# A linear-attention and SwiGLU block on one core: the first token tiles and first products put in one written order

## The chip, the cores and the metric

One core of a Trainium2 chip runs the whole kernel. The metric is device time in microseconds (us) of one execution. All input and output tensors are float32 in HBM.

## The reference

```python
x = A_x                                  # 2048 tokens x 1024
xn = _layernorm(x, axis=-1)
s = _A_ref(xn, A_wqkv, A_wo)             # linear attention, 32 heads of 32, phi(t) = elu(t) + 1
g = _silu(_B_ref(xn, B_w1, B_w3, B_w2))  # SwiGLU, hidden width 3584
return x + s * g
```

In the attention, `kv` and `z` are sums over all tokens of `phi(k) v` and `phi(k)`. The output for a query is `phi(q) kv / (phi(q) z)`, times `wo`.

## The kernel before, in words

**Products.** Each matrix product is done by a seven-product scheme on 2 x 2 blocks: the left operand (normalised, transposed tokens) is kept as the blocks and sums A11, A12, A22, S1, S2, S3, S4, and the right operand (weights) as B11, B21, B22, T1, T2, T3, T4. Every operand is a pair of rounded float32 numbers, a high part and a low part: `split` (lines 83 to 92) has ScalarE round the source into the high part and VectorE subtract it from the source into the low part. `mm3` (94 to 99) multiplies high by high, high by low and low by high, and `product` (378) does so for four blocks of the inner dimension: twelve matmuls of 128 x 512.

**Halves.** The tokens come in two halves of 1024. A half has eight row tiles of 128 tokens. In the first half, tiles 0 to 3 give the upper row of blocks (A11 and A12, in the buffers `xa`), and tiles 4 to 7 the lower row (in `xb`). Tile i and tile 4 + i together give S1, S2, S3 and S4 for 128 columns of each operand.

**The start of the first half** is what the change touches:

- `prepare_first` (168 to 180) loads tiles 0 to 3, takes each tile's mean and variance on VectorE (`moments`, with `gather`, bn_stats twice on 512 columns, and `spread`, 140 to 151, a chain of small instructions with one square root on ScalarE), normalises on VectorE (`normalise`, 154), and transposes the blocks on TensorE with `turn_into` (156 to 163): four 128 x 128 transposes into one PSUM bank, ScalarE writes the high part, VectorE the low part.
- `prepare_rest` (192 to 210) does tile 4 + i: load, moments, normalise on VectorE, then four sums of 128 x 512 on GpSimd (203 to 206: S1, S3, S2 and S4), then the five transposed blocks S2, S3, S1, A22, S4 by `turn_into`. `behind` keeps its first steps from being issued before earlier ones.
- `gemm` with `early=True` (399 to 469) is done for the keys and values of pairs 0 and 1, called k0, v0, k1 and v1 here: B11 by A11, a copy of that into `u` on ScalarE, then B21 by A12 into the same bank, and `use` (phi for keys, a copy for values). The products with S1 to S4 and A22 follow when all four pairs of tiles are done. The first of them is T2 by S2 of k0.
- `Operands` (287 to 364) loads and splits the weights. For the four early ones a first load `w0...` of 128 columns (330) gives B11 and B21. The later load of 256 columns, `w...` (301), goes into the pool `raw`, whose two buffers first hold the tiles `xa0` (0 and 1) and `xa1` (2 and 3). So k0's load waits until tiles 0 and 1 have been transposed for the last time, and v0's until tiles 2 and 3 have been.

**What sets the order.** Each engine runs its own instructions in the order in which they were put in its queue. In the kernel before the compiler's scheduler chooses that order from program order and its own estimate of the times, apart from `tc.issue_after`, which holds an instruction behind another. All loads here go through SyncE's queue (SP). There are eight PSUM banks: a transposed block holds one until its low part is done, and an early product holds one from its first matmul to its `use`.

The sums of keys by values are kept in `kvacc` (110), zeroed on VectorE at the start. They are first added to by line 515, long after the stretch described here.

Of the kernel before, what the change touches and what calls it, by code (L numbers as in the profile page):

```python
# [22 lines left out]
def tile_linear_attention_times_swiglu(  # L23
# [39 lines left out]
    nc.gpsimd.memset(gap, 0.0)  # L63

# [3 lines left out]
    JG, NT = 4, C // (2 * P)  # L68
    FB = [(0, 8), (8, 16), (16, 22), (22, 28)]
# [13 lines left out]
    def split(pair, src=None, bias=None):  # L83
# [4 lines left out]
        if bias is None:  # L88
            nc.scalar.copy(out=hi, in_=src)
            return nc.vector.tensor_sub(out=lo, in0=src, in1=hi.bitcast(F32))  # L90
# [19 lines left out]
    kvacc = st.tile([P, ND, P], F32, tag="kvacc", bufs=1, name="kvacc")  # L110
    nc.vector.memset(kvacc, 0.0)
# [10 lines left out]
    def load_rows(rows, name):  # L122

        t = praw.tile([P, 2, D], F32, tag="raw", name=name)
        for c, r0 in enumerate(rows):
            nc.sync.dma_start(out=t[:, c], in_=x[r0:r0 + P, :])
        return t

    def moments(xs, dst):

        bs = st.tile([P, 2, 2, nc.vector.BN_STATS_DIM], F32, tag="bs", name="bs")
        for c, t in enumerate(xs):
            gather(t, bs[:, c])
        spread(bs, dst)

# [4 lines left out]
    def spread(bs, dst):  # L140
        n = dst.shape[1]
# [4 lines left out]
        nc.scalar.activation(y, v, AF.Sqrt)  # L146
        nc.vector.reciprocal(y, y)
# [20 lines left out]
    def prepare_first(A, mom):  # L168

        xs = []  # L170
        for g in range(TH // 4):
            t = load_rows([(2 * g + e) * P for e in range(2)], f"xa{g}")
            xs += [t[:, e] for e in range(2)]
            for i in (2 * g, 2 * g + 1):
                moments(xs[i:i + 1], mom[:, i:i + 1])
                normalise(xs[i], mom[:, i])
                turn_into(A, {"A11": xs[i][:, :C]}, i, f"0_{i}")
        for i, t in enumerate(xs):
            _, low = turn_into(A, {"A12": t[:, C:]}, i, f"0_{i}")
        return xs, low  # L180

    def load_second(mom, g):

        ts = []
        for i in (2 * g, 2 * g + 1):
            ts.append(job_tile([P, D], f"xb{i}") if i < 3 else pb.tile([P, D], F32, tag="b", name=f"xb{i}"))
            nc.sync.dma_start(out=ts[-1], in_=x[C + i * P:C + (i + 1) * P, :])
        j = TH // 2 + 2 * g
        moments(ts, mom[:, j:j + 2])
        return ts  # L190

    def prepare_rest(A, mom, i, t0, seconds, behind):

        with ExitStack() as order:
            for mark in behind:
                order.enter_context(tc.issue_after(mark.ins))
            if i % 2 == 0:
                seconds += load_second(mom, i // 2)
            t1, s1 = seconds[i], small(f"S1x{i}")
            normalise(t1, mom[:, TH // 2 + i])  # L200

            a11, a12, a21, a22 = t0[:, :C], t0[:, C:], t1[:, :C], t1[:, C:]
            nc.gpsimd.tensor_add(out=s1, in0=a21, in1=a22)
            nc.gpsimd.tensor_sub(out=a21, in0=a11, in1=a21)
            nc.gpsimd.tensor_sub(out=a11, in0=s1, in1=a11)
            last = nc.gpsimd.tensor_sub(out=a12, in0=a12, in1=a11)
        behind.append(last)
        yield
        turned, _ = turn_into(A, {"S2": a11, "S3": a21, "S1": s1, "A22": a22, "S4": a12}, i, f"0_{i}")
        yield turned  # L210
# [76 lines left out]
    class Operands:  # L287
# [15 lines left out]
        def upto(self, n):  # L303
            while n not in self.B:
                next(self.stages)
            return self.B[n]
# [823 lines left out]
```

## Time and profile before

| | us |
|---|---|
| median of 3 runs (2372.07 to 2375.66) | 2372.78 |
| profiled execution, its own time | 2371.04 |
| span of the profiled execution | 2369.0 |
| TensorE busy in the span | 2329.2 |

Times in the rows count from the start of the span. In a row of the timeline stand the start, the duration, the engine (PE is TensorE's matmul, DVE is VectorE, ACT is ScalarE, POOL is GpSimd, SPq the queue of SyncE), the line, the operation, what it writes and reads with the shape, how many instructions are merged in the row, and in brackets the idle time of the engine before it and what ended it. Instructions overlap in an engine's pipeline: two starts on one engine lie closer than one duration.

### The profile page before, as it was taken

The page shows a single profiled execution, that of the slowest core. Times are in us where ns is not written, and L with a number is a line of the kernel's source. Part 1 is how long each engine was busy: PE and PEld are TensorE (multiplying, and loading weights), DVE is VectorE, ACT ScalarE, POOL GpSimd, SP SyncE. Part 2 cuts the span into 40 slices and gives each one's busy share as a digit, 9 for nine tenths or more (in the row PEclk, how much of TensorE's full clock was granted, in tenths as well). Part 3 has the DMA queues.
Part 4 walks back from the last instruction along what each step waited for, and adds up shares of the span by engine and source line. Part 5 has one row for each costly group of instructions (what it writes and reads, how often), then busy time and mean ns, then how long its engine had stood idle before and what let it go on. Part 6 is the DMA issues. An engine that isn't in the chain of part 4 may idle for free.

```text
span 2369.0 us, 29756 instructions
## 1 busy us (share of the span) xinstructions
PE 2329.2 (98%) x10544; PEld 1928.1 (81%) x10544; DVE 1635.7 (69%) x2906; ACT 940.7 (40%) x1595; POOL 330.7 (14%) x423
## 2 busy tenths in 40 slices
PE   6999999999999999999999999999999999999999
PEld 5788888888888888888788888888888888878777
DVE  8755687879788675657776877777636556676644
ACT  5433544443333244445434332333535233344532
POOL 3000111212121110000131312122100111210001
PEclk9999999999999999999999999999999999999999
DMA  3222444547666573334353555543636565665656
GB/s 125 89 98 81 169 147 165 196 156 249 226 236 232 173 291 114 121 118 140 135 184 132 195 179 184 172 150 119 229 97 222 151 187 183 192 199 158 190 147 151
DMA packets 264676, 395.48 MB, mean 167 GB/s; under 512 B 20944, under 2 KB 187088, under 8 KB 264080
## 3 DMA queue, kind: packets, MB, share of 16 engines
q1 hardware_dynamic: 230416, 293.12, 38.1%
q0 software_dynamic: 34112, 100.48, 12.2%
q8 instruction: 82, 1.34, 0.2%
q14 instruction: 66, 0.54, 0.1%
HBM read 271.58 MB, written 140.77 MB: 174 GB/s over the span
## 4 chain that ended last, share of the span: by engine, by line
PE 94%; DMA 3%; DVE 1%; POOL 1%; ACT 1%; issue 0%; SPq 0%; DVEq 0%; ACTq 0%; POOLq 0%
PE cB L99 3%; PE cB L97 3%; PE cB L98 3%; PE dB L99 2%; PE dB L97 2%; PE dB L98 2%; PE aB L99 2%; PE aB L98 2%; PE aB L97 2%; PE kv L514 1%; DMA XA12s<-qs_d 1%; PE cs L97 1%; PE cs L99 1%; PE cs L98 1%; PE den L754 1%; PE ds L98 1%
## 5 line engine op out<-in xcount | busy, mean ns | idle before, releaser
L636 POOL DMA_DIRECT2D ho_d<-hs x112 | 101.7, 908 | 84.5 <-DVE hs L609 62.0
L628 POOL DMA_DIRECT2D ho_d<-sg x56 | 51.1, 912 | 432.0 <-DVE sg L623 358.1
L787 POOL DMA_DIRECT2D qs_d<-qd x32 | 27.8, 874 | 457.7 <-DVE qd L611 430.2
L587 POOL DMA_DIRECT2D pq_d<-pq x32 | 17.6, 550 | 484.9 <-DVE pq L475 480.3
L962 DVE TENSOR_TENSOR acc<-cB,acc 128x512 f32<-128x512 f32 x73 | 50.2, 688 | 20.1 <-PE cB L99 20.0
L626 POOL DMA_DIRECT2D ho_d<-sg x56 | 37.9, 677 | 135.0 <-DVE sg L623 120.6
L915 DVE TENSOR_TENSOR XA12B<-XA12B 128x512 fp32r<-128x512 f32 (+1 forms) x32 | 19.7, 624 | 45.4 <-ACT XA12B L914 45.4
L962 DVE TENSOR_TENSOR acc<-dB,acc 128x512 f32<-128x512 f32 x53 | 36.5, 688 | 19.9 <-PE dB L99 19.7
L99 PE MATMUL cB<-T3B,XS3B 128*128 128x512 f32 x112 | 43.9, 392 | 1.0 <-DVE XS3B L915 1.0
L99 PE MATMUL cB<-T4B,XA22B 128*128 128x512 f32 x112 | 43.7, 391 | 0.6 <-DVE XA22B L915 0.6
L99 PE MATMUL dB<-T1B,XS1B 128*128 128x512 f32 x112 | 43.8, 391 | 0.4 <-DVE XS1B L915 0.4
L97 PE MATMUL cB<-T2B,XS2B 128*128 128x512 f32 x112 | 44.0, 393 | 0.2
L97 PE MATMUL cB<-T3B,XS3B 128*128 128x512 f32 x112 | 43.8, 391 | 0.3 <-ACT XS3B L914 0.3
L99 PE MATMUL dB<-B22B,XS4B 128*128 128x512 f32 x112 | 43.8, 391 | 0.0
L97 PE MATMUL cB<-T4B,XA22B 128*128 128x512 f32 x112 | 43.7, 391 | 0.0
L99 PE MATMUL cB<-T2B,XS2B 128*128 128x512 f32 x112 | 43.7, 390 | 0.0
L98 PE MATMUL cB<-T4B,XA22B 128*128 128x512 f32 x112 | 43.6, 390 | 0.0
L97 PE MATMUL dB<-T1B,XS1B 128*128 128x512 f32 x112 | 43.6, 390 | 0.0
L98 PE MATMUL dB<-B22B,XS4B 128*128 128x512 f32 x112 | 43.6, 390 | 0.0
L98 PE MATMUL cB<-T2B,XS2B 128*128 128x512 f32 x112 | 43.6, 390 | 0.0
L98 PE MATMUL cB<-T3B,XS3B 128*128 128x512 f32 x112 | 43.6, 390 | 0.0
L98 PE MATMUL aB<-B11B,XA11B 128*128 128x512 f32 x112 | 43.6, 390 | 0.0
(5749 smaller groups left out, 8043.1 us busy)
## 6 DMA issues: line engine op xcount, KB each, us to landing
ho_d<-hs POOLq DMA_DIRECT2D x112, 256.0 KB, 5.6
qs_d<-qd POOLq DMA_DIRECT2D x32, 512.0 KB, 4.1
ho_d<-sg POOLq DMA_DIRECT2D x56, 256.0 KB, 3.4
w<-in_B_w SPq DMA_DIRECT2D x56, 256.0 KB
wt_d<-w SPq DMA_DIRECT2D x28, 512.0 KB
pq_d<-pq POOLq DMA_DIRECT2D x32, 256.0 KB, 2.8
a_dS<-xo SPq DMA_DIRECT2D x16, 512.0 KB
pqd<-pq_d SPq DMA_DIRECT2D x16, 512.0 KB
```

The lines of the kernel that those rows point to most:

```text
L97: nc.tensor.matmul(acc, lhsT=wh, rhs=ah, start=start, stop=False, skip_group_check=True)
L98: nc.tensor.matmul(acc, lhsT=wh, rhs=al, start=False, stop=False, skip_group_check=True)
L99: return nc.tensor.matmul(acc, lhsT=wl, rhs=ah, start=False, stop=stop, skip_group_check=True)
L514: nc.tensor.matmul(acc, lhsT=r[:, 1, t], rhs=r[:, 0, t], start=t == 0, stop=t == C // P - 1)
L587: nc.gpsimd.dma_start(out=pq_d[j // JG][2 * h + c][:, j % JG], in_=pq)
L626: nc.gpsimd.dma_start(out=ho_d[i][2 * h + c][:, :, 0, k], in_=halves[:, :, 0])
L628: nc.gpsimd.dma_start(out=ho_d[i][2 * h + c][:, :, 1:3, k], in_=halves)
L636: nc.gpsimd.dma_start(out=ho_d[i][2 * h + c][:, :, 3 + 2 * e:5 + 2 * e, k], in_=o[e].rearrange("p (g n s) -> p g n s", n=2, s=P))
L754: nc.tensor.matmul(den[0], lhsT=zb[0][:, o:o + P], rhs=a[e][:, i], skip_group_check=True, start=j + e + i == 0, stop=j + e == ND - 1 and i ...
L787: nc.gpsimd.dma_start(out=qs_d[m][:, :, k], in_=t.rearrange("p a (n s) -> p (a n) s", s=P))
L915: return high, nc.vector.tensor_sub(out=lo, in0=src, in1=hi.bitcast(F32))
L962: evicted.append((1, nc.vector.tensor_add(out=to, in0=b, in1=to)))
```

## The change

The four early generators, the loads, the moments, the normalisation and the transposes of all eight tiles of the first half are written out in one function, `first_operands`, and the instructions of TensorE, ScalarE, VectorE and GpSimd in it are tied, engine by engine, to the order in which they are written (`as_written`; `IN_LINE` holds these four). Beside that:

- 40 transposes of the identity matrix stand first on TensorE.
- Tile 0 is loaded in two parts. The loads are ordered: tiles 0 to 3, w0 of k0, tiles 4 and 5, w0 of v0, tiles 6 and 7, w0 of k1, w0 of v1. The kernel before has the last two, w0 of v1 and tile 7, later.
- Moments are taken for two tiles in one chain of small instructions, with one more (`low`, minus mean times the reciprocal deviation), and ScalarE normalises in place, in halves of 512 columns for tiles 0 to 3 and 1024 columns at once for tiles 4 to 7.
- The low parts of k0's B21 and of v0's B11 and B21 are made by GpSimd. S1 of tiles 5 to 7 is added on VectorE, S1 of tile 4 on GpSimd as before.
- Tile 7 takes the place of `kvacc`, which is allocated and zeroed (on GpSimd) after the first operands.

```diff
+    warm = bank("warm")
+    for _ in range(40):
+        nc.tensor.transpose(warm[:, :P], ident, ident)
+    @contextmanager
+    def as_written():
+        traced, begin = nc.cur_bb.bb.instructions, len(nc.cur_bb.bb.instructions)
+        yield
+        last = {}
+        for i in traced[begin:]:
+            if i.engine in last and i.engine in IN_LINE:
+                tc.add_manual_dep(i, last[i.engine], mybir.DependencyInfo(
+                    mybir.DependencyClass.NoSync, mybir.DependencyReason.DATA))
+            last[i.engine] = i.name
...
-            return nc.vector.tensor_sub(out=lo, in0=src, in1=hi.bitcast(F32))
+            return low.tensor_sub(out=lo, in0=src, in1=hi.bitcast(F32))
...
+    def first_operands(A, m, o):
...
+        def weights(*names):
+            for g, n in names:
+                o[g].upto(n, nc.vector if (g, n) in ((0, "B11"), (2, "B11"), (2, "B21"), (3, "B11"), (3, "B21")) else nc.gpsimd)
+        def half_way(g):
+            found[g] = begin(bs[g], pair(g))
+        def finish(g):
+            root(pair(g), found[g])
+            nc.vector.scalar_tensor_tensor(low[:, 2 * g:2 * g + 2], pair(g)[:, :, 0], -1.0, pair(g)[:, :, 1],
+                                           op0=ALU.mult, op1=ALU.mult)
+        def normal(i, cols=slice(0, D)):
+            nc.scalar.activation(xs[i][:, cols], xs[i][:, cols], AF.Identity, bias=low[:, i:i + 1],
+                                 scale=mom[:, i, 1:2])
...
+        with as_written():
+            look(0, 1)
+            half_way(0)
+            look(2)
+            finish(0)
+            normal(0, L)
+            normal(1, L)
+            look(3)
+            half_way(1)
+            lay_first = [lambda i=i: lay(i, A11=x0[i][:, L]) for i in range(4)]
+            finish(1)
+            lay_first[0]()
+            normal(2, L)
+            normal(3, L)
+            lay_first[1]()
+            weights((0, "B11"))
+            lay_first[2]()
+            lay_first[3]()
+            next(m[0])
+            look(4, 5)
+            half_way(2)
+            for i in range(4):
+                normal(i, R)
+            weights((0, "B21"), (1, "B11"))
+            finish(2)
+            normal(4)
+            normal(5)
+            lay(0, A12=x0[0][:, R])
+            lay(1, A12=x0[1][:, R])
+            next(m[0])
+            lay(2, A12=x0[2][:, R])
+            lay(3, A12=x0[3][:, R])
+            next(m[1])
+            weights((1, "B21"))
+            first_sum(0, nc.gpsimd)
+            sums(0)
+            look(6, 7)
+            first_sum(1)
+            half_way(3)
+            next(m[0])
+            next(m[1])
+            finish(3)
+            normal(6)
+            normal(7)
+            sums(1)
+            weights((2, "B11"), (2, "B21"))
+            first_sum(2)
+            first_sum(3)
+            next(m[1])
+            lay_sums(0)
+            next(m[0])
+            next(m[2])
+            sums(2)
+            next(m[1])
+            lay_sums(1)
+            weights((3, "B11"), (3, "B21"))
+            next(m[2])
+            next(m[3])
+            sums(3)
+            lay_sums(2)
+            next(m[2])
+            next(m[3])
+            o[0].ask()
+            o[0].upto("T2")
+            next(m[2])
+            lay_sums(3)
+            next(m[3])
+            next(m[3])
...
         product(ba, B.upto("B11"), A["A11"], True)
+        if early:
+            yield
         copied = nc.scalar.copy(out=u, in_=ba)
         if early:
-            catch_up(copied)
             yield
             product(ba, B.upto("B21"), A["A12"], False)
+            yield
             use(0, 0, ba)
             yield
```

Here `look` is bn_stats (four instructions for two tiles), `half_way` and `finish` are the two parts of the chain of small instructions, `lay` is `turn_into`, `sums(i)` is S3, S2 and S4 of tile pair i on GpSimd, `lay_sums(i)` turns the five blocks of that pair, and the successive calls of `next(m[g])` are: B11 by A11, the copy, B21 by A12, `use`.

## Rows read from the trace of the kernel before

**Rows 1.** The page: busy time of each engine in the span.
```profile
PE 2329.2 (98%) x10544; PEld 1928.1 (81%) x10544; DVE 1635.7 (69%) x2906; ACT 940.7 (40%) x1595; POOL 330.7 (14%) x423
```

**Rows 2.** Waits of PE, whole span: waiter, releaser, us in total, times, longest.
```profile
PE tA L161 <- DVE v L145: 11.2, 1, 11.2
PE tS L161 <- POOL xa L205: 4.9, 4, 3.5
...
PE bv__803 L97 <- ACT T2v__706 L89: 3.0, 1, 3.0
...
PE tA L161 <- DVE xa L154: 1.7, 2, 0.9
```

**Rows 3.** Timeline of PE, 20 to 75 us.
```profile
20.14 0.48 PE L97 MATMUL ak__311<-A,B11k__304 128*128 128x512 f32 x1
...
36.37 0.39 PE L99 MATMUL av__334<-A,B21v__330 128*128 128x512 f32 x1
37.48 0.66 PE L161 MATMUL tS<-ident,xa 128*128 128x128 f32 x4 [0.72 <-POOL xa L205]
37.98 0.60 PE L161 MATMUL tS<-ident,xb 128*128 128x128 f32 x4
38.41 0.60 PE L161 MATMUL tS<-ident,S1x 128*128 128x128 f32 x4
...
54.44 1.12 PE L161 MATMUL tS<-ident,xa 128*128 128x128 f32 x4 [3.53 <-POOL xa L205]
55.34 1.06 PE L161 MATMUL tS<-ident,xb 128*128 128x128 f32 x4
...
58.45 0.50 PE L97 MATMUL bk__683<-S,T2k__669 128*128 128x512 f32 x1
...
66.38 0.39 PE L98 MATMUL ck__684<-S,T3k__673 128*128 128x512 f32 x1
66.61 0.39 PE L99 MATMUL ck__684<-S,T3k__673 128*128 128x512 f32 x1
69.99 0.50 PE L97 MATMUL bv__803<-S,T2v__706 128*128 128x512 f32 x1 [3.00 <-ACT T2v__706 L89]
```

**Rows 4.** Stretches: PE, PEld, DVE, ACT, POOL busy (count), granted clock, DMA.
```profile
54.00:58.40 4.40, 3.96 (x20) 3.73 (x20) 4.40 (x7) 2.28 (x5) 1.65 (x2) 0.61 0.00 0
71.00:75.00 4.00, 4.00 (x12) 3.12 (x11) 3.88 (x8) 2.88 (x5) 0.00 (x0) 0.57 0.05 18
```

**Rows 5.** Timeline of VectorE, 4 to 65 us.
```profile
4.31 1.29 DVE L138 BATCH_NORM_STATS2 bs<-xa 128x6 f32<-128x512 f32 x2 [1.41 <-DMA xa<-in_A_x]
...
30.86 0.16 DVE L147 RECIPROCAL y<-y 128x2 f32<-128x2 f32 x1
31.06 0.16 DVE L149 TENSOR_TENSOR u<-y 128x2 f32<-128x2 f32 x1
...
33.15 1.25 DVE L151 SCALAR_TENSOR_TENSOR mom<-u,y 128x2 f32<-128x2 f32 x1
34.43 3.54 DVE L154 TENSOR_SCALAR xb<-xb,mom 128x1024 f32<-128x1024 f32 x2
...
39.05 1.87 DVE L90 TENSOR_TENSOR S<-tS,S 128x512 fp32r<-128x512 f32 x3
...
54.98 1.30 DVE L90 TENSOR_TENSOR T1k__665<-wk__662,T1k__665 128x512 fp32r<-128x512 f32 x1
...
64.99 0.69 DVE L326 TENSOR_TENSOR wv__699<-wv__699 128x512 f32<-128x512 f32 x1 [2.71 <-DMA wv__699<-in_A_wqkv]
```

**Rows 6.** Timeline of GpSimd, 32 to 56 us.
```profile
32.60 1.78 POOL L203 TENSOR_TENSOR S1x<-xb 128x512 f32<-128x512 f32 x1 [31.22 <-DVE xb L154]
34.46 1.29 POOL L204 TENSOR_TENSOR xb<-xa,xb 128x512 f32<-128x512 f32 x1
...
54.46 1.27 POOL L206 TENSOR_TENSOR xa<-xa 128x512 f32<-128x512 f32 x1
```

**Rows 7.** Timeline of ScalarE, 30 to 59 us.
```profile
30.99 0.20 ACT L146 ACTIVATE y<-v 128x2 f32<-128x2 f32 x1 [0.18 <-DVE v L145]
...
32.43 1.28 ACT L474 ACT_TABLE_LOAD   x1
33.73 0.63 ACT L474 ACTIVATE pk<-pk 128x512 f32<-128x512 f32 x1
...
38.18 1.56 ACT L89 CAST S<-tS 128x512 fp32r<-128x512 f32 x3 [3.06 <-PE tS L161]
...
57.78 0.62 ACT L89 CAST T2k__669<-wk__662 128x512 fp32r<-128x512 f32 x1
58.30 0.62 ACT L89 CAST T3k__673<-wk__662 128x512 fp32r<-128x512 f32 x1
```

**Rows 8.** Timeline of SP's queue: DMA issues.
```profile
58.48 0.37 SPq L301 DMA_DIRECT2D wv__699<-in_A_wqkv  x1
```

More of the change, by code (lines that the diff above doesn't have):

```diff
@@ L1 @@
-from contextlib import ExitStack
+from contextlib import ExitStack, contextmanager
 from itertools import zip_longest
@@ L81, in tile_linear_attention_times_swiglu, with split @@
     a_d = {n: dram.tile([P, 2, ND // 2, C], F32, name=f"a_d{n}") for n in AOPS}
-    def split(pair, src=None, bias=None):
+    def split(pair, src=None, bias=None, low=nc.vector):
         hi, lo = pair[:, 0], pair[:, 1]
@@ L120, in job_tile @@
         return praw.tile(shape, F32, tag="job", bufs=3, name=name)
[L122 to L134, printed above, removed]
     def gather(t, bs):
@@ L140, in spread, with begin @@
     def spread(bs, dst):
+        root(dst, begin(bs, dst))
+    def begin(bs, dst):
         n = dst.shape[1]
@@ L146, in spread, with root @@
         nc.scalar.activation(y, v, AF.Sqrt)
+        return v, y, u
+    def root(dst, vyu):
+        v, y, u = vyu
         nc.vector.reciprocal(y, y)
@@ L166, in operand_tiles @@
         return {n: pa[n].tile([P, 2, ND // 2, C], FR, tag=n, name=f"{n}_{h}") for n in AOPS}
[L168 to L210, printed above, removed]
@@ L294, in __init__ @@
             self.w, self.c0, self.name, self.raw, self.next = w, c0, name, None, None
-            self.B, self.places = {}, {}
+            self.B, self.places, self.first, self.low = {}, {}, None, nc.vector
             self.stages = self.made(early)
@@ L301, in ask, with begin, upto @@
                 fetched[:] = [nc.sync.dma_start(out=self.raw, in_=columns(self.w, self.c0, 2 * P))]
-        def upto(self, n):
+        def begin(self):
+            self.first = pb.tile([P, ND, P], F32, tag="b", name=f"w0{self.name}")
+            nc.sync.dma_start(out=self.first, in_=columns(self.w, self.c0, P))
+        def upto(self, n, low=nc.vector):
             while n not in self.B:
+                self.low = low
                 next(self.stages)
@@ L320, in ready @@
                     place(n)
-                split(self.places[n], b[n])
+                split(self.places[n], b[n], low=self.low)
                 self.B[n] = self.places[n]
@@ L328, in made @@
             if early:
-                first = pb.tile([P, ND, P], F32, tag="b", name=f"w0{self.name}")
-                nc.sync.dma_start(out=first, in_=columns(self.w, self.c0, P))
-                halves(first)
+                halves(self.first)
                 ready("B11")
+                yield
                 ready("B21")
                 yield
+                self.low = nc.vector
             self.ask()
@@ L543, in half @@
         if h == 0:
-            mom = st.tile([P, TH, 2], F32, tag="mom", bufs=1, name="mom")
-            (xs, low), seconds = prepare_first(A, mom), []
-            behind = [low]
             m = [f(pair, early=True, own=pair == 0 and f is keys) for pair in range(2) for f in (keys, values)]
-            r = [prepare_rest(A, mom, i, xs[i], seconds, behind) for i in range(TH // 2)]
-            for i in range(4):
-                next(m[i])
-            for i in range(4):
-                next(r[i])
-            next(m[0])
-            next(m[1])
-            for i in (2, 3):
-                with tc.issue_after(next(r[i - 2]).ins):
-                    next(m[i])
-            next(r[2])
-            next(r[3])
+            first_operands(A, m, [ops[f"{n}0_{pair}_"] for pair in range(2) for n in "kv"])
+            kvacc.append(st.tile([P, ND, P], F32, tag="kvacc", bufs=1, name="kvacc"))
+            nc.gpsimd.memset(kvacc[0], 0.0)
         else:
```

51 lines of the change are left out of this document (47 added, 4 removed).

## The prediction

> **What bounds the kernel now.** The page comes first: TensorE is busy for 98% of the span [rows 1], so only its gaps and its slow stretches can be won. The list of TensorE's waits shows where they are: 11.2 us before its first instruction, 1.7 and 4.9 us in the preparation of the first half, and 3.0 us at the first product with v0's T2 [rows 2]. The remaining waits of the span are smaller. The timeline of TensorE then gives the order: first product at 20.14, six of the eight early products by 36.6, then transposes that each wait for GpSimd's sums, a gap of 3.5 us before the last tile at 54.44, T2 of k0 at 58.45, and the gap of 3.0 us before 69.99 [rows 3]. The stretches show a granted clock of 0.61 and 0.57 after those two gaps [rows 4]: part at 2.4 GHz, part at 1.2 GHz, with TensorE idle before each fall. That cost 4.4 x 0.39 = 1.7 us and 4.0 x 0.43 = 1.7 us. So the start of T2 of k0, 58.45, is the mark: before it all early products and all transposes are done, in both kernels, and the same work follows it. I work out that mark for the changed kernel, and then what of the later 3.0 + 1.7 us returns.
>
> **Paces used**, as start-to-start distances: a matmul 0.23, so 2.74 for a product; a group of four transposes 0.44 [rows 3]; a high part on ScalarE 0.48 from PSUM (three in 1.56) and 0.52 from SBUF [rows 7]; a low part on VectorE 0.60 (three in 1.87); bn_stats 0.60 (two in 1.29); a small dependent instruction 0.20 (reciprocal to multiply) [rows 5]; a sum on GpSimd 1.36 when started right behind another that took 1.29 [rows 6].
>
> **Part 1, to the first product: earlier.** VectorE starts about 3.6, since half a tile is enough (a whole tile lets it start at 4.31 [rows 5]). It does four bn_stats (2.4, plus 0.9 waiting for tile 1), the first small part (0.7), two bn_stats (1.2), five small ones (1.0), two more bn_stats (1.2), small part and root (1.0), five small ones (1.0): 13.0. Then ScalarE has two half normalisations, a cast of A11 and B11's cast, VectorE three lows and the last: first product at 17.2, 2.9 earlier than 20.14. The 40 transposes take under 40 x 0.22 = 8.8 us (0.22 from 55.34 - 54.44 for four, the slow pace [rows 3]) from about 1.4, and nothing of TensorE's is ready before 10: they cost nothing. The loads come early enough: every tile has a place of its own.
>
> **Part 2, the second halves: later.** Behind the last A11 low (17.1) VectorE's tied order has four bn_stats and the small part, to 20.2, and the square root for tiles 4 and 5 stands in ScalarE's queue ahead of the normalisation of the A12 columns. ScalarE therefore idles 16.0 to 20.3. From there it has 0.2 + four halves 2.08 + two weight casts 1.04 + tiles 4 and 5 at 0.95 each + four A12 casts and a copy 2.4: the last A12 cast at 28.0, its low at 28.8. v0's first product waits for GpSimd's low part of B11 (second in its queue, 23.2 + 1.36 + 1.3) until 25.9, and k0's second product starts at 28.9, as in the kernel before. By then three products have started there against two here. A 1024-wide normalisation on ScalarE has no row: its ends are 0.62 (one 512-wide, rows 7) and 1.24 (two); 0.95 lies by the longer one less one fixed part. The ends move the mark by -0.7 and +1.1.
>
> **Part 3, the moments of tiles 6 and 7: the port.** GpSimd runs without a pause from 28.6 (low part of v0's B21, S1 of tile 4, sums of tiles 4 and 5) to about 40, eight instructions of 1.36 and a little more. VectorE's bn_stats of tiles 6 and 7 end at 31.2, then S1 of tile 5, small part, root and reciprocal, to 33.1. Four small instructions with two SBUF inputs follow. In the kernel before, the one of them that met a GpSimd sum took 1.25 us in place of 0.15, ending 34.40, when GpSimd's sum ended (32.60 + 1.78 = 34.38); a low part from SBUF took 1.30 in place of 0.68 beside the sum from 54.46 to 55.73 [rows 5, 6]. The other three small ones have no row beside GpSimd: 0 or 1.25 each, and I take the waiting one, the nearest in shape and operands. So they start 33.1, 34.6, 36.0, 37.5 and ScalarE normalises tile 6 at 37.7, not at 33.9.
>
> The Trainium skill, page "SBUF — State Buffer", section "Who interferes with whom", says that a VectorE instruction with two SBUF inputs and a GpSimd instruction that reads SBUF shut each other out for the whole instruction, and that whoever starts second waits. By that rule all four wait and the mark is the 66.5 below; if it held only for the one with a row, 66.0, because the weights' lows would meet the sums instead.
>
> **Part 4, from there ScalarE's queue sets the end.** 37.7 + two normalisations 1.9 + two casts of k1's weights 1.04 = 40.6; the low of B11 is ready at 41.0, so k1's first product starts at 41.0, after TensorE has idled 4.2 us since the transposes of the first tile pair. ScalarE goes on: five casts 2.4, phi 0.64 + table load and exponential 1.9 (1.28 + 0.63 [rows 7]), a copy 0.5, five casts 2.4, a cast of v1's B11 0.5: 49.0. Its low stands on VectorE behind five lows of the second tile pair and one more wait for GpSimd: 51.6, TensorE idle for 4.0. From there TensorE alone sets the pace: v1's first product 2.74, transposes 2.2, k1's second 2.74, transposes 2.2, v1's second 2.74 = 12.6, plus 1.7 for the fallen clock after such a gap [rows 4], and 0.55 for the last tile's low: **66.5**, which is 8.0 later than 58.45. GpSimd's sums end near 51 (54.46 + 1.27 = 55.73 before), and are no longer what is last.
>
> **Part 5, what returns behind the mark.** v0's weights are loaded 58.48, when tile 3 has been turned, and 11.5 us later, at 69.99, the product with T2 can start [rows 8, 3]. In the changed kernel tile 3 is turned at 63.2, so that product could start at 74.7; T2, T3 and T1 of k0 last from 66.5 to 74.7. The 3.0 us go, and the 1.7 us of slow clock behind them. Ends: all of 4.7 or nothing.
>
> GpSimd's zeroing of the key-value sums (128 x 1024) costs nothing: GpSimd idles after its last sum, and line 515 needs the tile much later. It has no row; if someone waited for it, two sums' time, 2.7 us.
>
> **Sum.** +8.0 - 3.0 - 1.7 = +3.3 us on the profiled execution's 2371.04. The median of the runs is 1.7 above that execution, so on its scale 2372.8 + 3.3 = 2376.1. About 0.2%, 4.7 us, is what a measurement of this kernel tells from no change; the forecast lies within it.
>
> **Rivals.**
>
> *Slower: the low parts and first sums on VectorE also alternate with GpSimd's sums.* In part 4 I let k1's two lows and the two S1 of tiles 6 and 7 pass in one go, since GpSimd then waits for S1 of tile 6. If GpSimd has its sums of the next pair ready, each of the four takes 1.3 us more, and the five lows behind them with them: 66.5 + 4 to 6.7 = 70.5 to 73.2, or +7 to +10 after the return. It decides at 40 to 46 us. For it: the 3.54 us for two normalisations that needed 1.6 alone, alternating with GpSimd [rows 5]. Against it: the wait for S1 in GpSimd's own order.
> The Trainium skill's page "Perfetto Trace Analysis", section "Optimizing Scalar/DVE Operations", warns that moving work between GpSimd and VectorE might not help because they share a port; that speaks for this rival.
>
> *Faster: the ties bind less than I read.* TensorE then takes products between transposes as before, GpSimd's chain starts 28.6 in place of 32.6 and sets the end as now: mark 54.5, -4.0, and -1.7 more if the gap before the last tile, and with it the fall of the clock, goes. Time 2367 to 2369. For it: the sums did end last before [rows 2]. Against it: every engine named is chained.
>
> *No port cost at all.* The mark is 61.2 (-5.3), and the sum 2.8 - 4.7 = -1.9, still within 0.2%. The row of 1.25 us speaks against it.
>
> **How the numbers follow.** My own case with its bounds (mark 65.8 to 67.6, a part of the 3.0 us perhaps kept) has 0.40, the slower rival 0.33, the faster one 0.17, no port cost 0.10. The forecast's own range is 2374 to 2379. The range for 8 in 10 is 2367 to 2382: it takes in the faster rival's better end and most of the slower one. Faster by over 0.2%: the faster rival and a little, 0.20. Slower: the slower rival and my case where part of the 3.0 us stays, 0.37. The same: 0.43.
>
> **What the profile would show.** Right: first product near 17; ScalarE idle until the square root near 20; the small instructions for tiles 6 and 7 at some 1.3 us each; two gaps of about 4 us before the first products of k1 and v1, the clock down after them; the mark near 66; no wait at v0's T2. Wrong: small instructions at 0.2 us beside busy GpSimd, a mark below 62, or the 3.0 us wait still there.

## The result and the profile after

The change made the kernel slower: 2380.18 us (median of 8 runs, 2377.33 to 2384.18) against 2372.62 for the kernel before, run beside it on the same chip. The ratio is 1.0031 [1.0021, 1.0041], some +7.4 us. That is inside the range for 8 in 10 (2367 to 2382), just above the forecast's own range (2374 to 2379), and beyond the 0.2% that counted as no change; the forecast was +3.3. The profiled execution took 2380.8 us, with a span of 2379.0.

TensorE's busy time rose by 12.0 us, more than the span did, with 40 instructions more [rows 1 for before]:

```profile
PE 2341.2 (98%) x10584; PEld 1934.5 (81%) x10584; DVE 1631.0 (69%) x2891; ACT 948.9 (40%) x1605; POOL 331.3 (14%) x424
```

TensorE's waits up to 105 us (waiter, releaser, us in total, times, longest) answer to [rows 2]:

```profile
PE tA L170 <- ACT xa L215: 5.3, 2, 4.4
PE av__572 L114 <- ACT B11v__564 L106: 1.9, 1, 1.9
PE warm L66 <- POOL ident masks.py:199: 1.4, 1, 1.4
PE av__389 L114 <- ACT uv__388 L522: 1.4, 1, 1.4
PE av__389 L116 <- POOL B11v__349 L107: 1.3, 1, 1.3
PE av__572 L116 <- DVE B11v__564 L107: 1.3, 1, 1.3
PE ak__511 L114 <- ACT B11k__447 L106: 1.0, 1, 1.0
PE tA L170 <- ACT v L608: 0.9, 1, 0.9
```

The 4.9 us for GpSimd's sums and the 3.0 us for v0's T2 are gone. Of the 11.2 us at the start the 40 transposes fill 6.2 (1.43 to 7.60), and a wait of 4.4 us follows them. Instead the early products themselves wait, for casts, low parts and a copy, 1 to 2 us each. TensorE's timeline, in the order of [rows 3], shows where:

```profile
17.58 0.79 PE L114 MATMUL ak__317<-A,B11k__299 128*128 128x512 f32 x1 [0.69 <-ACT A L106]
...
25.52 0.50 PE L114 MATMUL av__389<-A,B11v__349 128*128 128x512 f32 x1 [0.37 <-ACT B11v__349 L106]
...
27.59 0.50 PE L116 MATMUL av__389<-A,B11v__349 128*128 128x512 f32 x1 [1.34 <-POOL B11v__349 L107]
...
35.87 0.50 PE L114 MATMUL av__389<-A,B21v__402 128*128 128x512 f32 x1 [1.36 <-ACT uv__388 L522]
...
42.05 0.50 PE L114 MATMUL ak__511<-A,B11k__447 128*128 128x512 f32 x1 [0.97 <-ACT B11k__447 L106]
...
50.87 0.50 PE L114 MATMUL av__572<-A,B11v__564 128*128 128x512 f32 x1 [1.86 <-ACT B11v__564 L106]
...
52.93 0.79 PE L116 MATMUL av__572<-A,B11v__564 128*128 128x512 f32 x1 [1.33 <-DVE B11v__564 L107]
...
66.62 0.39 PE L114 MATMUL bk__714<-S,T2k__643 128*128 128x512 f32 x1
...
78.45 0.39 PE L114 MATMUL bv__834<-S,T2v__737 128*128 128x512 f32 x1
```

First product 2.6 us earlier, the mark (T2 of k0) 8.2 us later, at 66.62, and no wait at v0's T2. The stretches (columns as in [rows 4]) show three slow ones at the start, at the first product of all, of v0 and of v1, and two more far behind, at 1155 us and, behind a wait of 2.08 us, at 2223 us:

```profile
17.60:21.80 4.20, 3.96 (x9) 2.78 (x10) 3.90 (x10) 0.39 (x2) 0.00 (x0) 0.50 0.67 201
27.60:32.00 4.40, 4.40 (x12) 3.52 (x13) 3.60 (x6) 3.06 (x7) 1.27 (x2) 0.61 0.00 0
50.80:56.00 5.20, 3.81 (x9) 2.77 (x10) 2.68 (x4) 1.02 (x3) 1.45 (x2) 0.67 0.52 177
...
1155.00:1159.50 4.50, 4.50 (x13) 3.57 (x14) 4.50 (x5) 0.00 (x0) 0.67 (x1) 0.62 0.07 29
...
2222.35:2226.85 4.50, 4.50 (x13) 3.54 (x14) 3.23 (x4) 3.53 (x6) 0.00 (x0) 0.62 0.05 18
```

VectorE's timeline answers to [rows 5]: the late second tile at the top, then the small instructions for tiles 6 and 7.

```profile
3.57 0.69 DVE L140 BATCH_NORM_STATS2 bs<-xa 128x6 f32<-128x512 f32 x1 [1.66 <-DMA xa<-in_A_x]
4.56 0.69 DVE L140 BATCH_NORM_STATS2 bs<-xa 128x6 f32<-128x512 f32 x1 [0.29 <-DMA xa<-in_A_x]
7.38 1.29 DVE L140 BATCH_NORM_STATS2 bs<-xa 128x6 f32<-128x512 f32 x2 [2.13 <-DMA xa<-in_A_x]
...
34.17 0.94 DVE L150 TENSOR_SCALAR v<-mom 128x2 f32<-128x2 f32 x1
35.38 0.17 DVE L156 RECIPROCAL y<-y 128x2 f32<-128x2 f32 x1 [0.27 <-ACT y L151]
35.58 0.87 DVE L158 TENSOR_TENSOR u<-y 128x2 f32<-128x2 f32 x1
36.48 0.16 DVE L159 SCALAR_TENSOR_TENSOR u<-u,v 128x2 f32<-128x2 f32 x1
36.68 1.15 DVE L160 SCALAR_TENSOR_TENSOR mom<-u,y 128x2 f32<-128x2 f32 x1
37.86 1.22 DVE L211 SCALAR_TENSOR_TENSOR low<-mom 128x2 f32<-128x2 f32 x1
```

GpSimd's timeline beside them, as in [rows 6]:

```profile
33.35 1.73 POOL L228 TENSOR_TENSOR xb<-xa,xb 128x512 f32<-128x512 f32 x1
35.16 1.27 POOL L229 TENSOR_TENSOR xa<-S1x,xa 128x512 f32<-128x512 f32 x1
36.51 1.29 POOL L230 TENSOR_TENSOR xa<-xa 128x512 f32<-128x512 f32 x1
37.77 1.29 POOL L228 TENSOR_TENSOR xb<-xa,xb 128x512 f32<-128x512 f32 x1
```

Each long one ends when a GpSimd sum ends: 35.11 and 35.08, 36.45 and 36.43, 37.83 and 37.80, 39.08 and 39.06. ScalarE's timeline ([rows 7]) shows its two roots and what waits behind the second, and the normalisation of tile 6:

```profile
21.41 0.20 ACT L151 ACTIVATE y<-v 128x2 f32<-128x2 f32 x1 [3.88 <-DVE v L150]
...
35.14 0.20 ACT L151 ACTIVATE y<-v 128x2 f32<-128x2 f32 x1 [4.48 <-DVE v L150]
35.25 0.57 ACT L522 COPY uv__388<-av__389 128x512 f32<-128x512 f32 x1
39.12 2.37 ACT L215 ACTIVATE xb<-xb,low,mom 128x1024 f32<-128x1024 f32 x2 [3.30 <-DVE low L211]
```

The load of v0's weights, on SP's queue, is issued 5.6 us later than in [rows 8] and is still early enough for T2 of v0:

```profile
64.08 0.37 SPq L403 DMA_DIRECT2D wv__730<-in_A_wqkv  x1
```

### The profile page after: what moved, and what is told of

The parts are those of the page before. It is cut to its first block, busy times and chain, and to the rows that moved or that the text cites. A ratio compares the mean times of both kernels' runs of the same rounds, so it can differ in the third digit from the quotient of the medians.

```text
span 2379.0 us, 29852 instructions
## 1 busy us (share of the span) xinstructions
PE 2341.2 (98%) x10584; PEld 1934.5 (81%) x10584; DVE 1631.0 (69%) x2891; ACT 948.9 (40%) x1605; POOL 331.3 (14%) x424
## 4 chain that ended last, share of the span: by engine, by line
PE 94%; DMA 2%; ACT 2%; DVE 1%; issue 0%; SPq 0%; DVEq 0%; ACTq 0%
PE cB L116 3%; PE cB L114 3%; PE cB L115 3%; PE dB L116 2%; PE dB L114 2%; PE dB L115 2%; PE aB L114 2%; PE aB L115 2%; PE aB L116 2%; PE kv L623 1%; DMA XA12s<-qs_d 1%; PE cs L114 1%; PE cs L116 1%; PE cs L115 1%; PE den L850 1%; PE ds L116 1%
## 5 line engine op out<-in xcount | busy, mean ns | idle before, releaser
L683 POOL DMA_DIRECT2D pq_d<-pq x32 | 17.6, 551 | 480.0 <-DVE pq L584 475.5
L114 PE MATMUL cB<-T2B,XS2B 128*128 128x512 f32 x112 | 43.9, 392 | 1.6 <-ACT cB L1055 1.5
L116 PE MATMUL dB<-B22B,XS4B 128*128 128x512 f32 x112 | 43.7, 390 | 0.0
L115 PE MATMUL cB<-T2B,XS2B 128*128 128x512 f32 x112 | 43.6, 389 | 0.0
L115 PE MATMUL dB<-B22B,XS4B 128*128 128x512 f32 x112 | 43.6, 389 | 0.0
L114 PE MATMUL dB<-B22B,XS4B 128*128 128x512 f32 x112 | 43.6, 389 | 0.0
L114 PE MATMUL aB<-B21B,XA12B 128*128 128x512 f32 x112 | 43.6, 389 | 0.0
```

The lines of the kernel that those rows point to most:

```text
L114: nc.tensor.matmul(acc, lhsT=wh, rhs=ah, start=start, stop=False, skip_group_check=True)
L115: nc.tensor.matmul(acc, lhsT=wh, rhs=al, start=False, stop=False, skip_group_check=True)
L116: return nc.tensor.matmul(acc, lhsT=wl, rhs=ah, start=False, stop=stop, skip_group_check=True)
L683: nc.gpsimd.dma_start(out=pq_d[j // JG][2 * h + c][:, j % JG], in_=pq)
```

## The experiments

Landmarks in all profiles, in us. "kv to den" goes from the last key-value product to the last denominator, "den to end" from there to the end of the span; "fall" says whether the granted clock drops behind a wait of 1.8 us near 1150 us that every kernel has (filled in the two named so). A ratio is to runs of the kernel before made beside that kernel, whose medians lie between 2372.34 and 2373.84, so it need not be the quotient of two medians of the table.

| kernel | first product | T2 of k0 | first kv product | kv to den | den to end | fall | median | ratio to before |
|---|---|---|---|---|---|---|---|---|
| before | 20.14 | 58.45 | 101.0 | 573.1 | 751.1 | no | 2372.62 | |
| before_again | 20.33 | 58.88 | 101.4 | 572.9 | 752.6 | no | | |
| before_warm | 19.72 | 58.43 | 98.2 | 574.7 | 753.5 | yes | 2372.39 | 0.9997 [0.9988, 1.0006] |
| before_delayed | 20.27 | 58.96 | 102.3 | 578.3 | 752.5 | no | 2377.34 | 1.0024 [1.0015, 1.0034] |
| after | 17.58 | 66.62 | 105.0 | 574.8 | 755.2 | yes | 2380.18 | 1.0031 [1.0021, 1.0041] |
| after_again | 17.56 | 67.64 | 106.1 | 575.2 | 751.5 | yes | | |
| whole_tile | 15.82 | 65.84 | 104.2 | 575.3 | 752.6 | yes | 2380.09 | 1.0035 [1.0023, 1.0046] |
| early_moments | 17.71 | 65.05 | 103.4 | 575.4 | 752.4 | yes | | |
| lows_on_vector | 17.94 | 69.54 | 107.9 | 573.4 | 754.9 | no | | |
| no_warm | 17.99 | 68.08 | 106.5 | 573.3 | 752.3 | no | 2379.06 | 1.0027 [1.0013, 1.0041] |
| filled | 17.30 | 67.51 | 105.8 | 572.7 | 753.9 | filled | 2377.31 | 1.0024 [1.0015, 1.0033] |
| untied | 23.95 | 58.72 | 96.8 | 575.2 | 754.4 | yes | 2372.35 | 0.9998 [0.9988, 1.0008] |
| reordered | 24.64 | 54.87 | 96.6 | 575.2 | 756.8 | yes | 2371.26 | 0.9995 [0.9986, 1.0004] |
| reordered_filled | 24.69 | 54.91 | 96.4 | 573.1 | 754.1 | filled | 2369.97 | 0.9990 [0.9982, 0.9999] |

Between the last denominator and TensorE's last products the granted clock falls in four profiles: after (at 2223 us, behind a wait of 2.08 us), reordered (2215, 2.27), untied (2076, 1.92) and lows_on_vector (2086, 1.88). These four have the longest last stretches, 754.4 to 756.8 us against 751.1 to 754.1 in the other ten. Such a late fall costs about 1.7 us (4.5 x 0.38 in the row at 2222 us).

**Both kernels once more**, unchanged, for the scatter of the landmarks.

> The kernel before once more, unchanged, for a second profile. T2 of k0 at 58.45 and the 3.0 us wait at v0's T2 should come again. Late falls of the clock: none if the first profile is typical (span 2369), one or two if they are a matter of the execution (span up to 2373).

> The changed kernel once more, unchanged, for a second profile. Between the start of T2 of k0 (66.6 us) and the first half's end it should repeat to half a microsecond. The first profile shows two falls of the granted clock late in the span (in the stretches from 1154 and from 2220 us) that the kernel before does not show there. If the written order of the start had moved something that far down, both falls come again at the same places (span 2379). If they are a matter of one execution, at least one is missing or elsewhere and the span differs by 1.5 to 3 us.

Single times 2374.45 and 2378.57. The wait at v0's T2 comes again (3.05 us), and no late fall is in the second profile of the kernel before. In that of the changed kernel the fall near 1150 us comes again and the one at 2223 us doesn't. Between two profiles of one kernel the mark moves by 0.4 and 1.0 us, and the time from the last denominator to the end by 1.5 and 3.7 us, of which the fall at 2223 us is about 1.7: of that last stretch one pair of profiles tells nothing below 4 us.

**The first tile in one load.**

```diff
-            step = C if i == 0 else D
+            step = D
```

> The changed kernel with tile 0 loaded in one piece, as in the kernel before. In the changed kernel tile 1 is waited for until 7.38 us, in the kernel before its first bn_stats is at 5.76. Theory: the two pieces, with one more issue ahead of the others, cost the DMA engines a dip between 4 and 7 us; then tile 1 is there at about 5.8, the first product starts near 16.3 and not 17.6, T2 of k0 is 1 to 1.4 us earlier (65.3) and the time 1 us less. Rival: the dip has another cause (the order of the later loads); then tile 1 stays at 7.4 and VectorE starts 0.7 us later than now, with T2 of k0 at 66.6 to 67.

The stretches from 4 us on (granted clock, DMA share and GB/s last), first of the changed kernel:

```profile
4.00:5.00 1.00, 1.00 (x8) 1.00 (x7) 0.71 (x2) 0.00 (x0) 0.00 (x0) 1.00 0.56 217
5.00:6.50 1.50, 1.50 (x16) 1.50 (x15) 0.26 (x1) 0.00 (x0) 0.00 (x0) 1.00 0.64 235
```

and of the one with a single load:

```profile
4.00:5.00 1.00, 1.00 (x7) 1.00 (x6) 0.62 (x2) 0.00 (x0) 0.00 (x0) 1.00 1.02 414
5.00:6.50 1.50, 1.50 (x15) 1.50 (x14) 1.50 (x4) 0.00 (x0) 0.00 (x0) 1.00 1.03 412
```

The split load halves the transfer rate for 2.5 us and makes the second tile late. Undone, the first product comes 1.8 us earlier, but the mark moves by 0.8 to 1.8 us only and the time not at all: the end of this stage isn't set by its beginning.

**The order untied**: the same steps, but the engines' queues are ordered by the planner, as in the kernel before.

```diff
-            if i.engine in last and i.engine in IN_LINE:
+            if False and i.engine in last and i.engine in IN_LINE:
```

> The changed kernel without the ties: the same instructions, written in the same order, but the scheduler may reorder them as in the kernel before. Theory (the written order keeps ScalarE idle before two square roots and TensorE idle before the first products of k1 and v1): T2 of k0 comes at 55 to 60, and the time is at or below that of the kernel before (2366 to 2373). Rival (the parts themselves cost, above all GpSimd's low parts and the normalisation on ScalarE): T2 of k0 stays at 64 or later and the time stays at 2377 to 2382.

The first product comes 6.4 us later and the mark 7.9 us earlier than in the changed kernel, and the time is that of the kernel before. So the written order, not the new operations, makes the loss: on balance they cost nothing when the queues are ordered otherwise. They don't gain either: the key-value stage starts 4.2 us before that of the shown profile of before, and the falls near 1150 and at 2076 us and a longer last stretch take that back.

**Tiles 6 and 7's moments earlier**, to tell whether the small operations at 34 to 39 us set the mark.

```diff
             finish(2)
+            look(6, 7)
+            half_way(3)
+            finish(3)
...
-            look(6, 7)
...
-            half_way(3)
...
-            finish(3)
```

> The moments, small parts and root of tiles 6 and 7 stand on VectorE and ScalarE right behind those of tiles 4 and 5, ahead of the normalisation of the second halves; nothing else is moved. Theory (the four small operations that alternate with GpSimd's sums, 34.2 to 39.1 us, delay the normalisation of tile 6, and with it k1's and v1's first products): at this earlier place GpSimd makes only low parts of weights, with pauses, so the small ones take 0.2 us or so each, and tiles 6 and 7 are normalised near 32 to 34 in place of 39.1. The second halves start up to 3 us later. T2 of k0 starts near 63, some 3 to 4 us before the changed kernel's 66.6. Rival A (TensorE alone sets the pace behind 50 us, or the second halves lose what tile 6 wins): T2 of k0 at 66 or later. Rival B (the start doesn't reach the end): T2 of k0 near 63, and the time still 2378 to 2381.

A single time, 2377.57. ScalarE normalises tile 6 at 32.40 instead of 39.12, 6.7 us earlier, and the mark comes at 65.05 where 63 was expected, 1.6 us earlier (2.6 against the second profile of the changed kernel). VectorE's timeline shows who took the rest:

```profile
32.15 1.67 DVE L225 TENSOR_TENSOR S1x<-xb 128x512 f32<-128x512 f32 x1
35.32 1.58 DVE L107 TENSOR_TENSOR B11k__447<-w0k__243,B11k__447 128x512 fp32r<-128x512 f32 x1 [1.50 <-ACT B11k__447 L106]
36.82 1.77 DVE L107 TENSOR_TENSOR B21k__450<-w0k__243,B21k__450 128x512 fp32r<-128x512 f32 x1
38.51 3.46 DVE L225 TENSOR_TENSOR S1x<-xb 128x512 f32<-128x512 f32 x2
...
48.67 1.55 DVE L107 TENSOR_TENSOR B11v__564<-w0v__245,B11v__564 128x512 fp32r<-128x512 f32 x1
```

The low parts of k1's weights and the first sums now meet GpSimd's sums and take 1.6 to 1.8 us each in place of 0.6 to 0.7. TensorE's timeline shows v1's first product, which starts 3.6 us earlier and then stands for its low part:

```profile
47.26 0.50 PE L114 MATMUL av__572<-A,B11v__564 128*128 128x512 f32 x1 [1.52 <-ACT B11v__564 L106]
...
50.27 0.80 PE L116 MATMUL av__572<-A,B11v__564 128*128 128x512 f32 x1 [2.28 <-DVE B11v__564 L107]
```

The theory is half right: the normalisation was late by the small operations, but behind it stands the same port. The slower rival of the prediction, which didn't come about in the changed kernel, is what happens here.

**All low parts on VectorE.**

```diff
-                o[g].upto(n, nc.vector if (g, n) in ((0, "B11"), (2, "B11"), (2, "B21"), (3, "B11"), (3, "B21")) else nc.gpsimd)
+                o[g].upto(n, nc.vector if True else nc.gpsimd)
```

> All low parts of the early weights are made on VectorE, in the places of the order where GpSimd made three of them; nothing else is moved. Theory (GpSimd's low part of v0's B11 held v0's first product by 1.3 us at 27.6, but tile 6's normalisation sets the rest): that wait goes, VectorE loses 3 x 0.6 us, and T2 of k0 starts 0 to 1.5 us earlier than 66.6. Rival (VectorE's queue is what everything waits for): T2 of k0 starts up to 2 us later.

A miss: the mark is 2.9 us later (1.9 against the second profile of the changed kernel), in a single time of 2382.27. In VectorE's fixed queue the two low parts of B21 and B11 wait for their casts until 25.35, ahead of the small operations of tiles 4 and 5, which end at 27.50 instead of 22.59; tiles 4 and 5 and the A12 columns are normalised and cast later by about 2. In these places of the order GpSimd's three low parts are worth about 2 to 3 us.

**Without the 40 transposes.**

```diff
-    warm = bank("warm")
-    for _ in range(40):
-        nc.tensor.transpose(warm[:, :P], ident, ident)
```

> The 40 transposes of the identity at the start are left out. Theory (they cost nothing and bring nothing, since TensorE idles from 7.6 to 12 us behind them and runs at half clock at its first product all the same): first product at 17.6, T2 of k0 at 66.6 within 0.5 us, time 2378 to 2381. Rival A (they bring something early): the first product takes longer than 4.3 us, and T2 of k0 is 1 us or more later. Rival B (the fall of the granted clock near 1150 us, which the four profiles with these transposes show and the two without don't, comes with them): the fall near 1150 us is gone, and the time is 1.5 to 2 us shorter.

First product 0.4 us and mark 0.4 to 1.5 us later, time 1.0027 against 1.0031: they cost nothing that these runs show. They do bring a little early: from the start of the first product to the transposes behind it takes 5.9 us without them (17.99 to 23.88) and 5.1 with them (17.58 to 22.71), the first sign of rival A; little of it is left at the mark. The fall near 1150 us is missing here, so the next two runs ask what it belongs to.

**The kernel before with the 40 transposes, and with a delay.** The second has this ahead of the first denominators, at 1067 us:

```diff
                 den.append(bank(f"den{c}"))
+                if c == 0:
+                    for _ in range(45):
+                        nc.tensor.transpose(den[0][:, :P], ident, ident)
```

> The kernel before with the changed kernel's 40 transposes of the identity at its start, and nothing else. Theory (the fall of the granted clock near 1150 us, seen in six of the eight profiles with these transposes and in none of the three without, is a matter of when TensorE comes to the 1.8 us wait, and the transposes have no part in it): start of T2 of k0 at 58.5 to 58.9, no fall near 1150 us, time equal to before within 0.2%. Rival (the transposes bring the fall, and with it the part of the loss that comes after 105 us): a fall near 1150 us, and the time 1.5 to 3 us longer than before.

> The kernel before with 45 extra transposes on TensorE ahead of the first product of the denominators, at 1067 us: about 4 us of TensorE's time (45 x 0.11, less the 1.0 us that it waits there), and nothing else. Theory (the wait of 1.8 us near 1150 us is followed by a fall or not by when it comes): it now comes 4 us later, as in the changed kernel, a fall follows it, and the time is 5 to 7 us longer than before. Rival (only the 4 us count): no fall, time 3.5 to 4.5 us longer.

Neither theory of the fall holds. The 4.5 us behind the wait, in stretches (granted clock third from the end), in the kernel before

```profile
1150.60:1155.10 4.50, 3.97 (x16) 3.01 (x17) 4.50 (x4) 0.92 (x3) 0.67 (x1) 1.00 0.09 33
```

with the 40 transposes

```profile
1148.50:1153.00 4.50, 4.41 (x12) 3.54 (x13) 4.50 (x5) 0.04 (x1) 0.67 (x1) 0.62 0.08 33
```

and with the delay

```profile
1157.60:1162.10 4.50, 3.93 (x16) 2.98 (x17) 4.50 (x5) 0.93 (x3) 0.67 (x1) 1.00 0.08 31
```

The fall comes with the transposes in the kernel before and not with the delay. The time of the kernel before stays the same with them, though its key-value stage begins 2.8 us earlier in the profile: the stage with the fall is 1.6 us longer, the last stretch 2.4.

A wait of 1.80 us in the same place is followed by a fall in 7 of the 12 profiles that have it: in 7 of the 8 whose kernel has the 40 transposes, and in none of the 4 without. (The expectation of before_warm says six of eight for what were six of seven at that time.) In both pairs of kernels that differ in them alone (before and before_warm, no_warm and after) the fall goes with them. That speaks for a part of the transposes in it, but lows_on_vector has them and no fall, and each kernel has one or two profiles; it isn't settled. The order of steps alone doesn't bring it, since before_warm has the order of before.

Of the delay the rival comes closer than the theory: no fall, and 5.0 us for its 3.5 to 4.5. At the last key-value product that profile is 2.1 us behind the shown one of before, at the first denominator 7.0, so 4.9 us were added in the middle, and the median is 5.0 us longer. A loss in the middle is passed on whole; for one at the start no run shows it by itself.

**The wait near 1150 us filled** with 18 transposes, in the changed kernel:

```diff
                 acc = bank(f"wp{j}_{n}")
+                if j + n == 0:
+                    for _ in range(18):
+                        nc.tensor.transpose(acc[:, :P], ident, ident)
```

> The changed kernel with 18 transposes into the bank of the first merged output weight, in the wait of 1.8 us near 1150 us that TensorE has there anyway. Theory (the fall of the granted clock behind that wait comes from TensorE's idling in it, and costs 1.7 us): the clock stays at 1.00 from 1145 to 1160 us, the last product of the denominators comes 1.7 us earlier against the key-value stage (574.6 us from the last key-value product to the last denominator in the changed kernel, 573.1 before), and the time is 1 to 2 us shorter than the changed kernel's: 2376.5 to 2379. Rival (the fall isn't the idling's, or the transposes delay what they stand ahead of): the fall stays, or the stage is no shorter.

As the theory expected. The stretch in its place has TensorE busy throughout, at 2.4 GHz:

```profile
1154.00:1160.00 6.00, 6.00 (x37) 5.20 (x36) 5.65 (x9) 1.92 (x4) 0.67 (x1) 1.00 0.10 37
```

From the last key-value product to the last denominator it takes 572.7 us, against 574.8 and 575.2, 2.1 to 2.5 us less. The ratio goes from 1.0031 to 1.0024, 1.7 us, which their intervals alone would not tell apart. In the table the stage takes 574.7 to 575.4 us in all seven profiles with a fall and 572.7 to 573.4 in those without (the delay apart): a fall there costs 2 us.

**Another tied order.** The first tile in one load, and the same steps moved so that what nobody waits for comes last. The body of `as_written` becomes:

```diff
-            step = C if i == 0 else D
+            step = D
...
+            look(0); look(1); half_way(0); o[0].upto("B11", nc.gpsimd); look(2); finish(0); normal(1, R); normal(1, L); normal(0, R); look(3); half_way(1)
+            normal(0, L); look(4); finish(1); lay(1, A11=x0[1][:, L]); normal(3, R); normal(2, L); normal(3, L); look(5); half_way(2); normal(2, R); finish(2)
+            lay(1, A12=x0[1][:, R]); o[2].upto("B11", nc.gpsimd); normal(4); look(6); first_sum(0, nc.vector); lay(0, A12=x0[0][:, R]); lay(0, A11=x0[0][:, L])
+            lay(3, A11=x0[3][:, L]); lay(2, A12=x0[2][:, R]); normal(5); first_sum(1, nc.vector); lay(2, A11=x0[2][:, L]); sums(0); lay(3, A12=x0[3][:, R])
+            o[1].upto("B11", nc.gpsimd); o[0].upto("B21", nc.vector); look(7); o[3].upto("B11", nc.vector); lay(0, S1=s1[0]); half_way(3); lay(0, S3=x1[0][:, L])
+            sums(1); lay(1, A22=x1[1][:, R]); finish(3); o[3].upto("B21", nc.vector); o[2].upto("B21", nc.vector); lay(1, S1=s1[1]); normal(6)
+            lay(0, S2=x0[0][:, L]); next(m[0]); next(m[2]); next(m[1]); first_sum(2, nc.vector); lay(1, S2=x0[1][:, L]); normal(7); lay(1, S4=x0[1][:, R])
+            next(m[3]); sums(2); next(m[3]); next(m[0]); lay(2, A22=x1[2][:, R]); o[1].upto("B21", nc.vector); next(m[1]); lay(2, S3=x1[2][:, L])
+            lay(1, S3=x1[1][:, L]); next(m[2]); first_sum(3, nc.gpsimd); next(m[3]); lay(0, S4=x0[0][:, R]); next(m[3]); lay(2, S4=x0[2][:, R]); next(m[2]); sums(3)
+            lay(2, S2=x0[2][:, L]); lay(0, A22=x1[0][:, R]); lay(2, S1=s1[2]); lay(3, S4=x0[3][:, R]); o[0].ask(); o[0].upto("T2"); lay(3, S1=s1[3])
+            lay(3, S2=x0[3][:, L]); next(m[0]); next(m[0]); lay(3, A22=x1[3][:, R]); next(m[1]); next(m[1]); next(m[2]); lay(3, S3=x1[3][:, L])
```

The second kernel has the 18 transposes besides.

> The changed kernel's steps in another tied order, with the first tile loaded in one piece. The order was worked out from the durations in the changed kernel's rows (0.6 us for a low part, 1.3 us for a small operation beside a GpSimd sum, and so on) so that the second halves of tiles 1 and 0 and the low parts of the next weights come before work that nobody waits for, and the first sums stand on VectorE. Theory (the start of T2 of k0 is a matter of the order of steps alone): T2 of k0 near 53.5 us, against 66.6 in the changed kernel and 58.45 before, T2 of v0 bound by its weights' load, which starts when tile 3 is turned, and the key-value stage begins 6 to 10 us before that of the kernel before; time 2362 to 2368. Rival A (the order found on paper meets waits that the rows don't show): T2 of k0 at 58 or later, time 2371 or more. Rival B (as with the order untied: what is won at the start is lost later): T2 of k0 near 53.5, the key-value stage earlier by 6 us or more, and the time still 2369 to 2373.

> The order worked out from the rows (the kernel named reordered) with the same 18 transposes in the wait near 1150 us. Theory (reordered begins the key-value stage 4.4 us before the kernel before, and loses 2.1 of it to the fall near 1150 us): time 2368 to 2370.5, 2 to 4 us less than before. Rival (what is won at the start is lost in the last stages all the same, by other waits): 2371 to 2373.

TensorE's timeline of the filled one:

```profile
24.69 0.49 PE L114 MATMUL ak__448<-A,B11k__258 128*128 128x512 f32 x1
...
54.91 0.48 PE L114 MATMUL bk__713<-S,T2k__631 128*128 128x512 f32 x1
...
57.50 0.50 PE L115 MATMUL bk__713<-S,T2k__631 128*128 128x512 f32 x1 [2.10 <-DVE S L107]
```

The first product comes 7.1 us later than in the changed kernel, TensorE then works for 11 us without a gap, and the mark comes 11.7 us earlier; the order of steps decides it, as the theory said (the single load alone moved the mark by 0.8 to 1.8). But the key-value stage begins only 4.6 us before that of the kernel before, not 6 to 10, since a wait of 2.1 us for a low part of the last tile stands right behind the mark, and the granted clock falls behind it (0.62 from 57.5 to 62 us, 1.7 us). So the 2362 to 2368 expected of reordered was missed: 2371.26, a time that both its rivals had, with the landmarks of neither. With the filled wait it is 2369.97, as expected there, 0.9990 [0.9982, 0.9999] of the kernel before. That one beats both kernels: the kernel before by 2.4 us, with an interval that ends just below 1, and the changed one by about 10.

## Why the prediction was right, and where it was not

The direction and the size at the mark were right; the likeliest class, no change, was not, and at +7.4 the time lies where the slower rival had it (+7 to +10), by another way than that rival's. By its steps:

- **Part 1** right: first product at 17.58 for 17.2. The second tile was awaited for 2.13 us where 0.9 was allowed, because the split load slows the transfers. The transposes at the start cost nothing, as costed. Not foreseen: that product ran at 1.2 GHz (0.50 from 17.6 to 21.8).
- **Part 2** right on ScalarE (idle 3.88 us until its root at 21.41; predicted until 20.3) and on the start of v0's product (25.52 for 25.9), late on what followed. (The kernel before had started four products by 28.9, not three: v1's first at 28.44.) That product stopped again at 27.59 for GpSimd's low part, which is second in its queue and ended at 27.53; k0's second product started at 31.21 for 28.9. A wait was missed altogether: v0's second product needs the bank that the copy `u` empties, and the copy stands behind ScalarE's root for tiles 6 and 7, at 35.25. A 1024-wide normalisation measured 1.14 us in the pair (from 39.12 to the next cast at 41.40), nearer its upper bound than the 0.95 taken.
- **Part 3** right in kind: three of the four small operations with two SBUF inputs took 0.87, 1.15 and 1.22 us, and one, which by the prediction waits as well, slipped between two sums in 0.16. The one with a single input took 0.94 as well, which wasn't costed. Tile 6 was normalised at 39.12 for 37.7. "No port cost" is out. By the Trainium skill, page "SBUF — State Buffer", section "Who interferes with whom", a VectorE operation with two SBUF inputs contends with a GpSimd instruction that reads SBUF, and whoever comes second waits for the whole instruction; the three long rows agree.
- **Part 4** right in its times, wrong on one of its two gaps: k1's first product at 42.05 for 41.0, but TensorE idled 0.97 us before it and not 4.2, since v0's second product, late by the copy, and the transposes behind it ran until 41.1, and no fall of the clock followed (1.00 from 42 to 46.5). v1's at 50.87 for 51.6, its three gaps 0.88 + 1.86 + 1.33 = 4.1 for 4.0, the clock at 0.67 behind them for 5.2 us (1.7, as priced). Mark 66.62 for 66.5. Some of this agreement is luck: delays in part 2 that weren't priced (the copy, the low part) fell into idle time that was. And the reading that ScalarE's queue sets the end from tile 6 on held only in part: 6.7 us there were worth 1.6.
- **Part 5** right: no wait and no fall at v0's T2. From the mark to the first key-value product it took 38.4 us for 42.55, so 4.2 of the 4.7 us returned.
- **The sum** is the step that fell short. +8.2 - 4.2 = +4.0 us arrived at the key-value stage in this profile (+5.1 in the second, both against the shown profile of before) where +3.3 was forecast. Then the sum ended, as if the 2270 us behind were alike. Between the two shown profiles they aren't: of the 10.0 us between their spans, 1.7 arise from the last key-value product to the last denominator and 4.1 behind that, with a fall of the clock in each part (1155 and 2223 us, about 1.7 us each) that the shown execution of before was spared. The fall near 1150 us stands in both profiles of the changed kernel and in neither of the kernel before, the later one in one of the four. The median's 7.4 [5.0, 9.7] can therefore be read in two ways: as the 4.0 to 5.1 us of the start and some scatter, or as these and the fall near 1150 us, 6 to 7 us, if most runs go as the profiles do. No run here tells the two apart: filling that wait won 2.1 to 2.5 us in its stage and 1.7 in the ratio, the latter within the noise. Without a fall in them the last 750 us still scatter from 751.1 to 754.1. Scatter goes with the clock in the runs without a profile too: 65 runs of the kernel before, made beside the experiments, have a span of 2369.4 us on average at a mean granted clock of 0.999 (9 runs), 2370.1 at 0.998 (44), 2371.6 at 0.997 (8) and 2374.4 at 0.996 (4). Why the same wait is followed by a fall in one profile and not in another is open.

The rivals: the slower one's mechanism didn't occur (the low parts at 42.03 and 42.64 took 0.69 and 0.68, the two first sums 1.28 together), but it appeared as soon as the order was changed (early_moments). The faster one, that the ties bind less than read, is what the untied order does at the mark (58.72), with the time that before has.

## What to carry to other kernels

An order tied by hand across four engines is only as good as its slowest meeting: an early first product is worth nothing (17.6, 15.8 and 24.7 us gave 2380, 2380 and 2370) if the later operands come in a chain. Cost each tied queue by who stands behind a waiting instruction, a copy behind a root and two-input VectorE work beside GpSimd sums above all. And when a delay is summed against one execution, look whether that execution was spared a clock fall that others show; a wait that can't be removed can be filled with work of TensorE's own.

## What the runs showed of the hardware that was not expected

- One 512 KB load cut into two halves lowered the DMA share from 1.02 to 0.56 and 0.64 for 2.5 us, with the same loads queued behind it.
- A small VectorE operation with one input (128x2, line 150) waited for GpSimd too: 0.94 us in the changed kernel and 1.08 and 1.19 in two experiments, in place of 0.17.
- The same 1.80 us of idle TensorE, after a stretch without a gap at 2.4 GHz, was followed by 4.5 us at 0.62 in 7 profiles and by no fall in 5; the 40 transposes at the start are in all of the 7 and in one of the 5. The Trainium skill, page "TensorE: Matmul & The Clock Gate", section "What's actually happening", has the chip look at activity in a window that runs freely of the kernel; that would let the moment decide, and no run here shows the window itself.
